# A gated mix of attention and feed-forward on one core: first transposing transfers whole, another duration and another set of weights in the planner

## The chip, the core and the metric

The kernel runs on one core of a Trainium2 chip. A core has a matrix engine (TensorE, in the profile PE, its weight loads PEld), a vector engine (VectorE, DVE), an activation engine (ScalarE, ACT), a general engine (GpSimd, POOL) and SyncE (SP), which here only issues transfers. Sixteen DMA engines move data between main memory and the on-chip memory. Results of PE land in PSUM, which the kernel uses as eight banks of 128 partitions by 512 float32 columns. The metric is the device time of one launch in microseconds.

## The reference

Sequence 2048, width 512, 32 heads of 16, feed-forward width 1792, all in bfloat16. The inputs named `B_x` and `A_x` are both given, and only `A_x` is read.

```
g = sigmoid((x * gate_w).sum(-1, keepdims=True))
q, k, v = split of x @ wqkv, 32 heads of 16
a = softmax(q @ k.T / 4) @ v, heads joined, @ wo
b = (silu(x @ w_gate) * (x @ w_up)) @ w_down
out = g * a + (1 - g) * b
```

The attention scores are 32 x 2048 x 2048 values, and each goes through an exponential. That is 2048 banks of 128 by 512.

## The kernel before, in words

**Units, slots and tiles.** The work of attention is cut into 32 units: a block of 512 queries and a group of four heads. A unit has 16 slots, one for each block of 128 keys. The scores of one slot are one tile: four banks, one for each of four heads. There are 512 slots, and `plan.slot` counts them.

**Two ways for a tile.** Most tiles are ACT's: PE computes two banks of scores (`score`), ACT takes the exponential of both in one instruction into `e_all` (`emit_group`, list `exps`), and PE multiplies the result by the values (`pv`), accumulating in one bank per unit. The other tiles are DVE's. It evicts the scores bank by bank with a multiplication and an addition into 16-bit integers whose bits read as a bfloat16 approximate an exponential (`emit_d`, tiles `c_t`; some lie in the space of `kaug` and `wd_t`). A sharper approximation needs several such images. With `groups[n] == 4` three shifted copies are made of the first (`copy`; the first of them on POOL, `lifted`), and PE makes four passes over the values. With `groups[n] == 2` two masks and a product are made (`bits`, `product`), and PE makes two passes. POOL can take a copy or a product from DVE (`take_over`), and works only beside certain instructions of DVE (`beside`).

**The planner.** The program is written by a planner in Python that runs when the kernel is built. It holds a clock for each engine (`plan.pe`, `plan.act`, `plan.dve`, `plan.pool`) and adds a fixed duration for each instruction that it emits. The order on every engine is the order of emission (`ordered`). `later(cost, f, ...)` puts a piece of DVE's work into the list `owed`, with the duration that the planner counts for it. `choose` picks which PSUM banks get the next group of scores, `v_unit` decides whether a tile of the present or next unit goes to DVE, `side` whether a piece of the projections or of the feed-forward goes to PE. The feed-forward, the projections of later units and the output run as such pieces beside attention.

**The weights.** These decisions are governed by 31 numbers. `begin(n)` replaces all of them at the slots that are keys of the table `WEIGHTS`:

```
HUNGRY, KEEP, FED, W3, W3T, W4, W4T, W4B, N1, N2, LOW, EXTRA, NEXT, SPARE, BURST, SHORT, BACK, FIRST, EB, OWN, NY, TAKE_C, TAKE_P, GLEAD, WINDOW, FACE, LATEST, SLACK, LEAD, LINE, STACK = WEIGHTS[n]
```

Until the first key, the constants at the head of the function hold. Those that the prediction names: `EB` is the number of pairs of banks in `e_all` after which PE must first multiply by values; `LEAD` is the time before the end of a unit's exponentials by which DVE must be able to begin a tile; `STACK` is the DVE work that may stand in the queue when another tile is taken; `TAKE_C` and `TAKE_P` let POOL take a copy or a product from DVE; `WINDOW` and `GLEAD` are the time that POOL must have for it.

**The start.** ACT's DMA queue loads 64 columns each of the weights and half of the plain rows of x; SP's loads the other rows and then issues the transposing transfers into `xT`, which holds x turned, in four chunks of 128 columns. For rows 0 to 1023 only chunks 0 and 1 come by such transfers; chunks 2 and 3 are turned by PE from the plain rows in `wd_t` (`turn`). Then come chunks 0 to 3 of rows 1024 to 2047. After these SP issues the rest of the value and projection weights. PE, after twelve matmuls that keep it going, turns its chunks, computes the keys and queries of the first unit in the order of chunks 3, 0, 2, 1 (rows 0 to 511, then 512 to 1023), bounds the scores, and starts with the first scores. The keys of rows 1024 to 2047 follow as planned pieces (`k0_pieces`).

**The gate.** `gate_end`, a piece at about slot 106, takes the exponential of 128 by 16 numbers on ACT and then has five small operations on DVE.

Of the kernel before, what the change touches and what calls it, by code (L numbers as in the profile page):

```python
# [82 lines left out]
def kernel(  # L83
# [13 lines left out]
    P = 128  # L97
    x = A_x.flatten_outer_dims()
# [6 lines left out]
    DC = D // P  # L105
    FC = F // P
    KT = S // P
    QBW = 512
# [10 lines left out]
    EB = 9  # L119
# [143 lines left out]
    def act(out, in_, **kw):  # L263
        ordered(nc.scalar.activation(out=out, in_=in_, **kw), [in_, *kw.values()], [out])  # L264
# [17 lines left out]
    queue = Ordered(nc.sync)  # L282


    xT = big.tile([P, DC, S], BF16, name="xT")
    wd_t = big.tile([P, FC, D], BF16, name="wd_t")
    HALF = DC // 2
    x_rows = wd_t[:, 0:4, :].rearrange("p f d -> p (f d)").rearrange("p (i d) -> p i d", d=HALF * P)
    def rows(q, t0):
        q.dma_start(out=x_rows[:, TQ * t0:TQ * t0 + TQ, :], in_=x[t0 * QBW:(t0 + 1) * QBW, HALF * P:D].rearrange("(i p) d -> p i d", p=P))  # L290

    def turned(dc, t0, n):
        queue.dma_start_transpose(out=xT[:, dc, t0:t0 + n * QBW], in_=x[t0:t0 + n * QBW, dc * P:(dc + 1) * P])

    rows(queue, 0)
    for t0 in (0, QBW):
        for dc in range(HALF):
            turned(dc, t0, 1)
    for dc in range(DC):
        turned(dc, 2 * QBW, 2)  # L300
    wqk = big.tile([P, DC, 2 * D], BF16, name="wqk")
    for c0 in (D, 0):
        if c0 == 0:
            rows(nc.scalar, 1)
        nc.scalar.dma_start(out=wqk[:, :, c0:c0 + 64],
                            in_=A_wqkv[:, c0:c0 + 64].rearrange("(dc p) c -> p dc c", p=P))
# [5 lines left out]
    for c0 in (D, 0):  # L312
        queue.dma_start(out=wqk[:, :, c0 + 64:c0 + D],
                          in_=A_wqkv[:, c0 + 64:c0 + D].rearrange("(dc p) c -> p dc c", p=P))
# [98 lines left out]
    plan = Plan()  # L413
# [4 lines left out]
    held = [None] * NP  # L418

    LANDED = 6.9  # L420
    FLIP, UNIT_US, PIECE_US, COLS_US, TURN = 0.1055, 0.2157, 0.0024, 0.2133, 0.0105
    TO_ACT, ACT_FIX, ACT_COL, ACT_IN = 0.485, 0.064, 0.4265, 0.167
    ACT_PE, DVE_PE, PE_DVE, ACT_DVE = 0.055, 0.08, 0.24, 0.06
    GPS = 1
    OWN = 0
    POOL_IN, POOL_FIX, POOL_ONE, POOL_PE, POOL_OVER = 0.12, 0.12, 0.43, 0.2, 0.1
    TAKE_P = 1
    FACE = 1
    TAKE_C = 1
    GLEAD = 5.771  # L430
    SLACK = 0.04
    LEAD = 7.615
    LINE = 1.3
    STACK = 4.9
    WINDOW = 1.503

    def spend(mode, mms, ready=0.0):

        plan.seq += 1
        work_at.append((plan.pe, mms))  # L440
        plan.pe = max(plan.pe + (FLIP if mode != plan.mode else 0.0), ready) + (TURN if mode == "C" != plan.mode else 0.0) + (0.226 * mms if mode == "F" else PIECE_US + COLS_US * mms)
        plan.mode = mode

    def later(cost, f, ready=None, key=None, fast=False):

        c = plan.chain
        if c is not None:
            c.owed += 1
        ready = plan.pe + PE_DVE if ready is None else ready
        owed.insert(sum(o[0] <= ready for o in owed), (ready, cost, f, c, key, fast))  # L450
# [318 lines left out]
    def gate_end():  # L769
        act(out=ge[:, :], in_=ge[:, :], func=ACT.Exp, scale=-1.0)  # L770
        plan.act += 0.2

        def end():
            vec.tensor_scalar(out=omg[:, :], in0=ge[:, :], scalar1=1.0, scalar2=None, op0=ALU.add)
            vec.reciprocal(gval[:, :], omg[:, :])
            vec.tensor_tensor(out=omg[:, :], in0=ge[:, :], in1=gval[:, :], op=ALU.mult)
            vec.reciprocal(odds[:, :], ge[:, :])
            wide.append(work.tile([P, QBW], BF16, tag="rd", name="rd")[:, :].bitcast(F32))
            vec.tensor_copy(out=wide[0][:, 0:P], in_=ident[:, :])
        later(0.5, end, plan.act + ACT_DVE, fast=True)  # L780
# [94 lines left out]
    def e_run(w):  # L875

        used = set(e_slot.values())
        for k in range(NE):
            i = (e_next[0] + k) % NE
            if i + w <= NE and not any(j in used for j in range(i, i + w)):  # L880
                return i
        return None
# [15 lines left out]
    def choose():  # L898
# [51 lines left out]
        left = (hi[au] - at_) * 4 - quarter  # L950
        if left >= 4 and len(e_slot) // 2 + 2 <= EB and e_run(4) is not None and not exps:
            for n in range(min(want, 2) + 1):
# [145 lines left out]
    def home_at(n):  # L1098

        short = n // KT > closed and any(v > 0 and m // KT == closed for m, v in needs.items())  # L1100
        return sorted(c_free)[1 if short else 0]
# [110 lines left out]
    def until(n):  # L1212

        un = n // KT
        return plan.act + (hi[au] - at_) * TILE_US + (hi[un] * TILE_US if un > au else 0.0)

    def take_over():

        seen = set()
        for i, (_, _, _, n, _, what) in enumerate(vops):  # L1220
            first = n not in seen
            seen.add(n)
            if what is None or n // KT < au:
                continue
            if what[0] == "P" and TAKE_P and first and n not in jobs and plan.dve + 2 * NV * WINDOW + GLEAD <= until(n):
                _, h, y = what
# [3 lines left out]
                return n  # L1230
            if what[0] == "C" and TAKE_C and what[1] == 2 and plan.dve + (NV + (len(jobs[n][4]) if n in jobs else 0)) * WINDOW + GLEAD <= until(n) and home_at(n) <= plan.dve:
                _, k, h, y = what
# [546 lines left out]
    for qb in range(QB):  # L1779
        for b in range(NB):  # L1780
# [21 lines left out]
            for g in {max(2 * b, 1), 2 * b + 1}:  # L1802
                q_of[UNIT.index((qb, g))] = q
    gates = [pace.add([(0.2, gate_end, False)], 40, 106, v_rest)]
    turned = pace.add([(1, turn_odds, True, "F", None)], 40, 130, gates, 2)
    need.setdefault(160, []).append(turned)

    def first_loads():
# [130 lines left out]
    def begin(n):  # L1939
        nonlocal HUNGRY, KEEP, FED, W3, W3T, W4, W4T, W4B, N1, N2, LOW, EXTRA, NEXT, SPARE, BURST, SHORT, BACK, FIRST, EB, OWN, NY, TAKE_C, TAKE_P, GLEAD, WINDOW, FACE, LATEST, SLACK, LEAD, LINE, STACK  # L1940
        plan.slot = n
        if n in WEIGHTS:
            HUNGRY, KEEP, FED, W3, W3T, W4, W4T, W4B, N1, N2, LOW, EXTRA, NEXT, SPARE, BURST, SHORT, BACK, FIRST, EB, OWN, NY, TAKE_C, TAKE_P, GLEAD, WINDOW, FACE, LATEST, SLACK, LEAD, LINE, STACK = WEIGHTS[n]
        for c in need.get(n, []):
            force(c)
        if n == 3:
            queue.dma_start(out=gw_col[:], in_=gate_w.rearrange("(dc p) -> p dc", p=P))
        if n == 28:
            late_loads()
        i = n - (QB + 1) * KT - 8  # L1950
        if 0 <= i < 2 * FC and i % 4 == 0:
            wd_due.append(i // 2)
        while wd_due and (wd_due[0] >= 4 or not wd_home[0]):
            wd_load(wd_due.pop(0))
        for f in at.pop(n, []):
            f()
        pace.begin_slot(n)
# [43 lines left out]
    def next_pv():  # L2001
        flush_act()
        while not pv_list(None):
            if d_wait:
                pay_d()
            elif vops and c_ready() < 1e9:
                pay_v()
            elif owed:
                pay()
            elif workable(1e8) is not None:  # L2010
                lifted(workable(1e8))
            elif asides:
                aside_now()
            else:
                lone_d()
        emit_pv(pv_list(None)[0])
# [19 lines left out]
    def v_unit():  # L2036
# [4 lines left out]
        while vu < UNITS:  # L2041
# [3 lines left out]
            if vu >= au and left > 0 and (vu or hi[0] > KT // 2):  # L2045
                end = plan.act + (left - 1) * TILE_US + ((hi[au] - at_) * TILE_US if vu > au else 0.0)
                busy = sum(v[0] for v in vops) + 0.6 * len(owed) + sum(d[3] for d in d_wait)
                if plan.dve + busy + (LEAD if vu < UNITS - 1 else LAST) <= end:
                    return vu
# [32 lines left out]
    while au < UNITS:  # L2082
# [5 lines left out]
        back = len(e_slot) // 2  # L2088
        if back >= EB or e_run(3) is None:
            next_pv()  # L2090
# [10 lines left out]
        if room > 0.02:  # L2101
# [4 lines left out]
            col = c is not None and (c.pieces[c.i][3:] or "C")[0] == "C"  # L2106
            urgent = c is not None and c.deadline < 0 and back < EB - 4
            visit = len(n_pv) + (len(c.pieces) - c.i if col else 0)
            going = col and 0 < c.i and len(c.pieces) < SHORT and back < EB - BACK
            if n_pv and fits > 0 and not urgent and not going and (plan.mode == "C" or visit > 1 and fits > 1 and (pv_turn[0] or c is None or col)  # L2110
# [119 lines left out]
```

## Time and profile before

| | |
|---|---|
| median of 3 runs | 746.43 us (746.19 to 746.45) |
| profiled execution | 747.79 us |
| its span, first to last instruction | 746.1 us |
| ACT busy | 731.5 us, 98% |
| PE busy | 731.6 us, 98% |
| DVE busy | 712.9 us, 96% |
| POOL busy | 281.6 us, 38% |
| granted clock of PE | 1.00 |

A row of the profile's groups reads: line, engine, operation, tile written and tiles read with their shapes, count, then busy time in us and mean duration of one in ns, then the idle time of the engine just before them and what ended it. Busy time of a group is a union: instructions of one engine overlap, so the mean times the count can be more. A row of the chain of waits reads: start, length, what. Nearly all instructions have the line of a helper (L261 for PE, L264 for ACT, L277 for the others), so groups are told apart by their tiles.

### The profile page before, as it was taken

The numbers are of one execution on the slowest core, as the hardware profiler recorded it, in microseconds if no ns is written. First come the engines' busy times: TensorE is split into PE (matmuls) and PEld (weight loads), VectorE is DVE, ScalarE is ACT, GpSimd is POOL, SyncE is SP. The second block draws the span as 40 slices with busy tenths as digits, with TensorE's granted clock in tenths as the row PEclk, the third lists the DMA queues.
The fourth block names the chain that finished last, engine by engine and source line by source line (L and its number), as shares of the span: only waits on it lengthen the run. The fifth ranks groups of instructions, "written<-read, shape, count | busy, mean of one in ns | idle before, by whom it ended". The sixth has DMA issues, their size and how long they took to land.

```text
span 746.1 us, 24177 instructions
## 1 busy us (share of the span) xinstructions
PE 731.6 (98%) x10198; PEld 238.8 (32%) x10198; DVE 712.9 (96%) x1175; ACT 731.5 (98%) x828; POOL 281.6 (38%) x400
## 2 busy tenths in 40 slices
PE   7999999999999999999999999999999999999997
PEld 3333233333333333333333333333332333333332
DVE  6799999999999999999999999999999999999995
ACT  5999999999999999999999999999999999999996
POOL 7034432442533412544323444442245235443320
PEclk9999999999999999999999999999999999999999
DMA  9010211353220003131100131211000132100011
GB/s 197 10 44 15 58 30 35 68 136 73 65 49 14 8 20 96 45 71 38 38 17 13 40 102 36 64 35 46 18 26 16 48 94 60 33 17 16 14 31 37
DMA packets 91685, 34.92 MB, mean 47 GB/s; under 512 B 75761, under 2 KB 91129, under 8 KB 91577
## 3 DMA queue, kind: packets, MB, share of 16 engines
q1 hardware_dynamic: 89320, 32.79, 18.6%
q8 instruction: 80, 1.31, 0.8%
q10 hardware_dynamic: 2256, 0.59, 0.4%
q14 instruction: 29, 0.23, 0.1%
HBM read 21.55 MB, written 2.35 MB: 32 GB/s over the span
## 4 chain that ended last, share of the span: by engine, by line
ACT 57%; PE 32%; DVE 6%; SPq 1%; issue 1%; DMA 1%; POOL 0%; DVEq 0%; POOLq 0%
ACT e_all L264 55%; PE psum L261 32%; DVE c_t L277 4%; ACT th L264 2%; SPq L277 1%; DMA xT<-in_A_x_dram 1%; DVE kaug L277 1%; DVE mt L277 1%; DVE gs L277 0%; DMA wu<-in_B_w_up_dram 0%; DVE on L277 0%; DMA on<-osb 0%; DVE osb L277 0%; POOL c_t L277 0%; DVEq L2225 0%
## 5 line engine op out<-in xcount | busy, mean ns | idle before, releaser
L264 ACT ACTIVATE e_all<-psum 128x1024 bf16<-128x1024 f32 (+1 forms) x755 | 706.7, 1103 | 2.6 <-PE psum L261 2.4
L277 DVE TENSOR_SCALAR c_t<-psum 128x512 uint16<-128x512 f32 x454 | 300.9, 684 | 8.6 <-PE psum L261 6.8
L261 PE MATMUL psum<-qx,kaug 32*128 32x512 bf16 (+1 forms) x1632 | 243.1, 385 | 4.2 <-ACT e_all L264 2.9
L277 POOL TENSOR_TENSOR c_t<-c_t,lift 128x256 int32<-128x256 int32 (+1 forms) x162 | 114.7, 716 | 169.3 <-DVE c_t L277 129.0
L261 PE MATMUL psum<-e_all,vaug 128*32 128x512 bf16 (+3 forms) x1992 | 164.9, 332 | 0.0
L261 PEld LDWEIGHTS <-kaug 32*128 32x128 bf16 (+1 forms) x2048 | 74.6, 91 | 262.2 <-ACT e_all L264 181.1
L261 PE MATMUL psum<-c_t,vaug 128*32 128x512 bf16 (+3 forms) x1856 | 144.1, 332 | 0.6 <-DVE kaug L277 0.3
L261 PEld LDWEIGHTS <-vaug 128*32 128x32 bf16 x4144 | 98.8, 95 | 125.5 <-issue 86.0
L277 DVE TENSOR_SCALAR c_t<-c_t 128x2048 uint16<-128x2048 uint16 (+2 forms) x194 | 131.5, 685 | 1.1
L277 POOL TENSOR_TENSOR c_t<-c_t 128x256 bf16<-128x256 bf16 (+3 forms) x62 | 53.9, 882 | 82.6 <-DVE c_t L277 57.4
L261 PE MATMUL psum<-xT,wg 128*32 128x512 bf16 x896 | 73.6, 383 | 0.1
L261 PE MATMUL psum<-wd_t,mt 128*32 128x512 bf16 x896 | 72.9, 383 | 0.0
L261 PE MATMUL psum<-xT,wu 128*32 128x512 bf16 x896 | 71.7, 383 | 0.1
L261 PE MATMUL psum<-q,kaug 32*128 32x512 bf16 (+1 forms) x256 | 48.6, 385 | 0.1
L277 POOL TENSOR_TENSOR kaug<-c_t,lift 128x256 int32<-128x256 int32 (+1 forms) x38 | 26.3, 701 | 43.2 <-DVE c_t L277 35.2
L261 PE MATMUL psum<-xT,wqk 128*32 128x512 bf16 x512 | 41.0, 383 | 0.2 <-DVE c_t L277 0.2
L277 DVE TENSOR_SCALAR kaug<-psum 128x512 uint16<-128x512 f32 x60 | 39.9, 680 | 0.8 <-PE psum L261 0.7
L277 DVE TENSOR_TENSOR c_t<-c_t 128x2048 bf16<-128x2048 bf16 (+1 forms) x32 | 39.1, 1222 | 0.0
L277 DVE SCALAR_TENSOR_TENSOR gs<-th,psum 128x512 bf16<-128x512 bf16 x56 | 37.9, 677 | 1.2 <-ACT th L264 1.1
L277 DVE SCALAR_TENSOR_TENSOR mt<-gs,psum 128x512 bf16<-128x512 bf16 x56 | 37.9, 677 | 1.0 <-PE psum L261 0.5
L264 ACT ACTIVATE th<-psum 128x512 bf16<-128x512 f32 x56 | 37.8, 674 | 0.0
L277 POOL TENSOR_TENSOR aq<-aq,kb 128x256 bf16<-128x256 bf16 x32 | 19.5, 612 | 47.4 <-DVE c_t L277 36.7
(127 smaller groups left out, 480.0 us busy)
## 6 DMA issues: line engine op xcount, KB each, us to landing
wg<-in_B_w_gate_dram SPq DMA_DIRECT2D x56, 128.0 KB
wu<-in_B_w_up_dram SPq DMA_DIRECT2D x56, 128.0 KB
on<-osb SPq DMA_DIRECT2D x120, 16.0 KB
rb<-rr SPq DMA_DIRECT2D x15, 128.0 KB
wd_t<-in_B_w_down_dram SPq DMA_DIRECT2D x7, 256.0 KB
qx<-qst SPq DMA_DIRECT2D x96, 16.0 KB
qx<-aq SPq DMA_DIRECT2D x96, 16.0 KB
out_dram<-o_t SPq DMA_DIRECT2D x12, 128.0 KB
```

The lines of the kernel that those rows point to most:

```text
L261: return ordered(nc.tensor.matmul(out, lhsT=lhsT, rhs=rhs, **kw), [lhsT, rhs], [out])
L264: ordered(nc.scalar.activation(out=out, in_=in_, **kw), [in_, *kw.values()], [out])
L277: return ordered(f(*a, **kw), reads, [out])
```

## The change

Three parts. The first four transposing transfers, 512 rows each, become two of 1024 rows; the four that follow stay as they are, so that SP issues six instead of eight. The planner counts 1.1 us instead of 0.5 for the five operations of the gate's end on DVE; the operations stay. The table of weights is another: 96 tuples, the first at slot 4, instead of 54 from slot 8; three tuples (at 88, 184 and 344) are in both tables. The opening constants `EB`, `GLEAD` and `LEAD` differ, too.

```
-    EB = 9
+    EB = 8
...
-    WEIGHTS = {8: (0, 0, 5.918, -0.267, -0.106, 0.5, 0.1, 0.1, 5.912, 0.508, 1.233, 0.818, 1.035, 0.271, 8.958, 18, 2, 0.339, 8, 1, 3, 0, 1, 0, 1.3, 0, 0.64, 0.02, 5.778, 1.771, 4.9),
...
+    WEIGHTS = {4: (0.08, 2, 4.965, -0.428, 0.009, 4, 0.248, 0.189, 6.643, 2.494, 1.557, 0.742, 0.94, 0.637, 8.802, 12, 2, 0.171, 8, 0, 3, 1, 1, 5.099, 1.444, 1, 0.605, 0.036, 7.295, 1.3, 4.9),
+        8: (0.08, 2, 4.965, -0.493, 0.009, 4, 0.302, 0.189, 6.643, 2.494, 1.557, 0.742, 0.898, 0.637, 8.802, 12, 2, 0.022, 8, 1, 3, 1, 1, 5.099, 1.444, 1, 0.605, 0.036, 7.295, 1.3, 4.9),
...
-    def turned(dc, t0, n):
-        queue.dma_start_transpose(out=xT[:, dc, t0:t0 + n * QBW], in_=x[t0:t0 + n * QBW, dc * P:(dc + 1) * P])
-
     rows(queue, 0)
-    for t0 in (0, QBW):
-        for dc in range(HALF):
-            turned(dc, t0, 1)
-    for dc in range(DC):
-        turned(dc, 2 * QBW, 2)
+    for t0 in (0, 2 * QBW):
+        for dc in range(DC if t0 else HALF):
+            queue.dma_start_transpose(out=xT[:, dc, t0:t0 + 2 * QBW], in_=x[t0:t0 + 2 * QBW, dc * P:(dc + 1) * P])
...
-    GLEAD = 5.771
+    GLEAD = 4.671
     SLACK = 0.04
-    LEAD = 7.615
+    LEAD = 7.295
...
-        later(0.5, end, plan.act + ACT_DVE, fast=True)
+        later(1.1, end, plan.act + ACT_DVE, fast=True)
```

The means over slots 8 to 511, each tuple held until the next key, of the fields that the prediction uses: `LEAD` 5.61 before and 4.50 after, `STACK` 4.72 and 5.39, `TAKE_C` 0.38 and 0.53, `TAKE_P` 0.91 and 0.81, `WINDOW` 1.48 and 1.30.

2 lines of the change are left out of this document (1 added, 1 removed).

## The prediction

> **What bounds the kernel now.** I read the page's totals first, then the busy time of the long middle stage, then the chain of waits, then the groups of instructions kept apart by shape, and last the first 20 us instruction by instruction.
>
> ```profile
> PE 731.6 (98%) x10198; PEld 238.8 (32%) x10198; DVE 712.9 (96%) x1175; ACT 731.5 (98%) x828; POOL 281.6 (38%) x400
> ```
>
> ```profile
> 20.00:737.00 717.00, 711.55 (x9993) 229.88 (x9994) 696.94 (x1126) 716.69 (x807) 267.17 (x368) 1.00 0.18 43
> ```
>
> The totals don't separate PE, ACT and DVE. The stage row does (columns: stretch and length, then busy time and count of PE, PEld, DVE, ACT, POOL, then granted clock, DMA share, GB/s). Between 20 and 737 us ACT is busy 716.69 of 717.00 us, so 0.31 us of it is idle. DVE has 20.06 us idle there.
>
> ```profile
> 31.73 0.51 ACT mt L264
> ...
> 389.54 39.35 ACT e_all L264 x43
> 428.88 0.10 issue
> 428.98 1.08 ACT e_all L264
> 430.06 0.49 ACT th L264
> ```
>
> A busy engine can still be stretched by waits inside its instructions; these chain rows (start, time, what) say it isn't. 43 exponentials in a row end every 39.35 / 43 = 0.915 us, and a tanh of the feed-forward part adds 0.49.
>
> ```profile
> L264 ACT ACTIVATE e_all<-psum 128x1024 bf16<-128x1024 f32 x749 | 700.4, 1098 | 2.6 <-PE psum L261 2.4
> L264 ACT ACTIVATE e_all<-psum 128x1536 bf16<-128x1536 f32 x6 | 9.7, 1623 | 0.0
> L277 DVE TENSOR_SCALAR c_t<-psum 128x512 uint16<-128x512 f32 x452 | 298.5, 681 | 8.6 <-PE psum L261 6.8
> L277 DVE TENSOR_SCALAR kaug<-psum 128x512 uint16<-128x512 f32 x60 | 39.9, 680 | 0.8 <-PE psum L261 0.7
> L277 DVE TENSOR_SCALAR wd_t<-psum 128x512 uint16<-128x512 f32 x16 | 10.7, 681 | 0.2 <-PE psum L261 0.2
> L277 DVE TENSOR_SCALAR c_t<-psum 128x1024 uint16<-128x1024 f32 x2 | 2.4, 1221 | 0.0
> ```
>
> The exponentials are divided between two engines. ACT takes 749 x 2 + 6 x 3 = 1516 banks of 512 columns. DVE takes 452 + 60 + 16 + 2 x 2 = 532 banks, which is 133 tiles of four. Together they are 2048 banks, all of them. So ACT's length is set by one number, how many tiles the planner gives to DVE. One tile more on DVE takes two double exponentials from ACT: 2 x 0.915 = 1.83 us. Nothing else in the middle stage can move the time by more than the 0.31 us that ACT idles, unless it makes ACT wait anew.
>
> The rest is 20 us at the start and 9 at the end:
>
> ```profile
> 7.85 1.30 SPq L277
> ...
> 9.20 1.30 SPq L277
> ...
> 10.54 5.40 DMA xT<-in_A_x_dram
> ...
> 15.98 0.96 PE psum L261 x10
> ...
> 16.96 14.77 ACT e_all L264 x16
> ```
>
> ```profile
> 1.33 1.23 SPq L277
> ...
> 2.61 1.25 SPq L277
> ...
> 3.90 1.26 SPq L277
> ...
> 5.20 1.26 SPq L277
> ```
>
> The chain begins with SP issuing eight transposing transfers one after another. The last is issued from 10.54 us, its data are whole at 15.94, PE stands until then, and ACT stands for PE.
>
> **The change, part by part.** *First transfers whole.* The first four transposes (512 rows each) become two of 1024 rows. A short one costs SP 1.23 to 1.26 us to issue, a long one 1.30 (rows above), so the issue price hardly knows the size. Four short ones occupy 1.33 to 6.47; two long ones would need 2 x 1.34 = 2.68, and every later issue on SP moves up by about 5.18 - 2.68 = 2.5 us. Behind them on SP stand the other four transposes and then the loads of the value and projection weights, which also move up. What the last landing is worth is bounded by who waits:
>
> ```profile
> 11.93 2.99 ACT L264 ACTIVATE e_all<-psum 128x1024 bf16<-128x1024 f32 x3 [0.17 <-PE psum L261]
> 16.96 14.77 ACT L264 ACTIVATE e_all<-psum 128x1024 bf16<-128x1024 f32 x16 [2.04 <-PE psum L261]
> ```
>
> ACT stands still for 2.04 us; that is the most this part can give, even though the issue moves by 2.5. Against it stands the earlier use:
>
> ```profile
> 6.19 0.45 PEld L261 LDWEIGHTS <-wd_t 128*128 128x128 bf16 x8 [0.16 <-DMA wd_t<-in_A_x_dram]
> 7.23 2.76 PE L261 MATMUL psum<-xT,mt 128*128 128x512 bf16 x16 [0.42 <-ACT xT L264]
> ```
>
> ```profile
> 4.00:6.00 2.00, 2.00 (x14) 1.01 (x12) 1.45 (x7) 0.68 (x3) 1.96 (x9) 1.00 1.26 216
> 6.00:8.00 2.00, 1.58 (x16) 0.91 (x14) 1.86 (x3) 1.42 (x3) 1.72 (x8) 1.00 0.90 155
> ```
>
> At 7.23 us PE starts on the transposed x and runs 16 matmuls without a stop. With whole transfers its second and fourth matmul need data of rows 512 to 1023 to have landed as well. The DMA engines are full at that time (share 1.26, then 0.90), and the doubled packets also sit beside the load of plain rows that PE waits for at 6.19. I bound the delay of the first exponential by 0 and by 0.7 us (half of the 1.3 us that one long transfer occupies) and take 0.2. If the last landing moves up by only half of 2.5 us, 1.25 are won instead of 2.04. So the start gives between -2.04 and +0.7; I take -1.5, nearest to the row of ACT's wait less the small delay.
>
> One rule speaks against that part. The Trainium skill, "DMA: Bandwidth & Descriptors", section "Issuing engines are not separate DMA queues", says that all issuers feed the same 16 engines and that the sequencer's time to start a transfer is usually small beside the transfer. By that, the saved issues would bring nothing here, the sum would lack the 1.5 us, and the time would be 742.6. The issue rows above show 1.23 to 1.30 us each and back to back, so I hold the queue of issues to be the limit, with the full DMA share as the reason for a doubt.
>
> *Gate's end.* The planner counts 1.1 us of DVE instead of 0.5 for five small operations:
>
> ```profile
> 167.18 0.16 DVE L277 TENSOR_SCALAR omg<-ge 128x16 f32<-128x16 f32 x1
> ...
> 168.00 0.68 DVE L277 TENSOR_SCALAR c_t<-psum 128x512 uint16<-128x512 f32 x1
> ```
>
> ```profile
> 170.00:175.00 5.00, 4.80 (x6) 1.00 0.00 0
> ```
>
> They held DVE from 167.18 to 168.00, 0.82 us. The instructions are the same after the change; only the order planned around them moves. The later stall that can be charged to it is the 0.20 us that ACT idles in 170 to 175. Worth 0 to -0.2; I take -0.1. What covers it otherwise is the stock of banks in front of ACT.
>
> *Buffers at the outset.* EB 8 for 9 holds only until the first tuple, at slot 4, and the opening constants are otherwise those of before except for two lead times. Nothing in the first stall depends on them: 0.
>
> *The weights.* They say how many tiles go to DVE and what a tile costs there.
>
> ```profile
> L261 PE MATMUL psum<-e_all,vaug 128*32 128x512 bf16 x1108 | 107.3, 383 | 0.0
> L277 DVE TENSOR_SCALAR c_t<-c_t 128x2048 uint16<-128x2048 uint16 x189 | 129.5, 692 | 1.1
> L277 DVE TENSOR_SCALAR kaug<-c_t 128x2048 uint16<-128x2048 uint16 x34 | 23.4, 690 | 0.1
> L277 DVE TENSOR_SCALAR c_t<-kaug 128x2048 uint16<-128x2048 uint16 x30 | 20.8, 697 | 0.2
> L277 DVE TENSOR_TENSOR c_t<-c_t 128x2048 bf16<-128x2048 bf16 x31 | 38.0, 1227 | 0.0
> L277 POOL TENSOR_TENSOR c_t<-c_t 128x512 bf16<-128x512 bf16 x22 | 25.4, 1156 | 22.3 <-DVE c_t L277 18.5 <-DVE kb L277 2.2 <-DMA on<-osb 1.3
> L277 POOL TENSOR_TENSOR c_t<-c_t 128x256 bf16<-128x256 bf16 x38 | 25.3, 670 | 56.8 <-DVE c_t L277 38.8 <-DVE kaug L277 15.5 <-DVE aq L277 2.0
> ```
>
> The four eviction rows further up (351.5 us), the three copy rows here (173.7) and the product row (38.0) make 563.2 us for 133 tiles, 4.2 us of DVE each. DVE's 20.06 idle microseconds hold at most 20.06 / 4.2 = 4.8 more tiles if nothing gets cheaper. Holding each tuple until the next key, I average the fields over slots 8 to 511, from the diff: LEAD, the time before a unit's end at which no further tile may be taken, falls from 5.61 to 4.50 us; STACK, the DVE work that may be queued, rises from 4.72 to 5.39; TAKE_C, POOL taking over a copy that costs DVE 0.69 us, is on in 53% of the slots instead of 38%; WINDOW, what POOL's share must fit, falls from 1.48 to 1.30. All four let DVE start more tiles or do them cheaper. TAKE_P, POOL taking over a product of 1.23 us, goes the other way, from 91% to 81%.
>
> No row shows how many tiles come of this. The bounds are +5 (all idle time of DVE, with a copy or two on POOL) and, below, -3 (the ten products that POOL does now in the two rows above, (22 x 2 + 38) / 8, all back on DVE: 10 x 1.23 / 4.2). I take +2: about half of the idle time (10 us, 2.4 tiles), since much of the other half is DVE's wait for PE before evictions (6.8 + 0.7 + 0.2 us in the eviction rows), which the weights needn't lift. That is -2 x 1.83 = -3.7 us. On PE a tile costs one or three more passes against the values; a pass is four matmuls side by side of 0.38 us (the PE row), so two tiles cost at most 6 x 0.38 = 2.3 us, and PE has 717.00 - 711.55 = 5.45 us idle in the stage row.
>
> *Sum.* -1.5 - 0.1 - 3.7 = -5.3 us. The profiled execution took 747.79 us (span 746.1), 1.36 more than the median 746.43; it may have had a longer wait at the start than the timed ones, which is a second reason to take 1.5 of 2.04. On its own time the sum gives 742.5, on the median 741.1.
>
> **The rivals.** *Transfers bound the start, not issues.* For it: the DMA share of 0.90 to 1.26 in the rows above. Against it: long issues at an even 1.34 us spacing. The start then gives 0: 746.43 - 3.8 = 742.6.
>
> *The division stays at 133.* For it: ACT without a gap and DVE with only 2.8% idle leave little. Against it: four fields loosened. Only the start and the gate count: 746.43 - 1.6 = 744.8.
>
> *DVE's tiles get dearer, slower.* With TAKE_P off in more slots, products come back from POOL to DVE, 1.23 us each. Seven of them, 8.6 us, cost DVE two tiles, and ACT 3.7 us: 746.43 - 1.6 + 3.7 = 748.5. It decides once more than six come back, with no other gain: (1.6 + 1.5) / 1.83 = 1.7 tiles, 7.1 us of DVE, 5.8 products. For it: POOL products fill 50.7 us of those two rows today, so there is something to lose. Against it: TAKE_C moves work the other way.
>
> **How the numbers follow.** Forecast 0.45; transfer-bound start with two tiles 0.17; division unchanged 0.14; dearer tiles 0.20; one tile fewer, 746.6, 0.04. A measurement of this kernel can tell about 0.2%, 1.5 us, from no change: faster is below 744.9, slower above 747.9. Unchanged division lies on that bound; I give 0.08 of it to faster and 0.06 to same. Faster 0.45 + 0.17 + 0.08 = 0.70, same 0.10, slower 0.20. Low end: five tiles and the whole wait, 746.43 - 9.2 - 2.0 = 735.2. High end: two tiles fewer, 748.5. Outside I leave about 0.15: three or more tiles fewer 0.10, more than five tiles 0.05.
>
> **What would show it.** The eviction rows should add up to about 540 banks instead of 532, and the double exponentials to about 745 instead of 749. SP's issues should show six transposes, the last from about 8 us, and ACT's idle time before the exponential now at 16.96 should fall from 2.04 to about 0.5. ACT should stay busy for all but a few tenths of the middle stage. The prediction is wrong if ACT idles there by more than a microsecond, if the count of banks on DVE falls, or if the first exponential comes more than 0.7 us after 11.93.

## The result, and the profile after

The changed kernel takes 745.09 us (median of 20 runs), the one before 746.28 us beside it: a ratio of 0.9986, 95% interval 0.9980 to 0.9992. That is 1.2 us faster, 0.14%, within the 0.2% that the prediction calls no change. The forecast was 5.3 us. A second series with the same kernel (`after_again`) gave 745.07 against 746.29 (0.9983, 0.9974 to 0.9991), so the 1.2 us is firm. One of the twenty runs of the kernel before took 1543 us and stands outside the ratio.

The profiled executions differ by more: 747.79 us (span 746.1) before, 745.10 (span 743.4) after. The one of before was 1.5 us above its median, the one after lies on it. What the two traces differ by at the start is therefore not what the timed runs differ by.

The stage rows of the kernel after (stretch, length, busy time and count of PE, PEld, DVE, ACT, POOL, clock, DMA share, GB/s), then its groups by shape:

```profile
20.00:733.00 713.00, 710.02 (x10038) 231.00 (x10034) 697.43 (x1126) 712.83 (x801) 272.87 (x388) 1.00 0.18 43
```

```profile
L264 ACT ACTIVATE e_all<-psum 128x1024 bf16<-128x1024 f32 x747 | 696.1, 1080 | 0.3 <-PE psum L261 0.2
L264 ACT ACTIVATE e_all<-psum 128x1536 bf16<-128x1536 f32 x6 | 9.2, 1540 | 0.0
L277 DVE TENSOR_SCALAR c_t<-psum 128x512 uint16<-128x512 f32 x462 | 308.1, 684 | 7.4 <-PE psum L261 5.3
L277 DVE TENSOR_SCALAR kaug<-psum 128x512 uint16<-128x512 f32 x64 | 42.6, 684 | 0.4 <-PE psum L261 0.2
L277 DVE TENSOR_SCALAR wd_t<-psum 128x512 uint16<-128x512 f32 x8 | 5.4, 683 | 0.1
L277 DVE TENSOR_SCALAR c_t<-psum 128x1024 uint16<-128x1024 f32 x1 | 1.2, 1220 | 0.0
```

ACT is still busy without a gap, 712.83 of 713 us. It takes 747 x 2 + 6 x 3 = 1512 banks instead of 1516; DVE takes 462 + 64 + 8 + 2 = 536 instead of 532. So the new table gives DVE 134 tiles: one more, not two.

The start after, as ACT, SP and PE show it (start, length, what, idle time before):

```profile
1.34 9.90 SPq L277 DMA_TRANSPOSE xT<-in_A_x_dram  x6
11.28 0.58 SPq L277 DMA_DIRECT2D rb<-in_A_wqkv_dram  x1
```

```profile
4.12 3.08 SPq L277 DMA_TRANSPOSE xT<-in_A_x_dram  x1
```

```profile
7.34 0.62 PE L261 MATMUL psum<-ident,wd_t 128*128 128x128 bf16 x8 [0.26 <-DMA wd_t<-in_A_x_dram]
7.80 2.80 PE L261 MATMUL psum<-xT,mt 128*128 128x512 bf16 x16
```

```profile
12.53 17.52 ACT L264 ACTIVATE e_all<-psum 128x1024 bf16<-128x1024 f32 x19 [0.16 <-PE psum L261]
```

Six issues take SP 9.90 us (9.57 to 9.98 in the six executions with two whole transfers and all loads); the eight of before took 10.50. The two saved issues are nearly all eaten by one: the third holds SP for 3.08 us instead of 1.30. (In `t_only`, below, it is the second, with 2.60 us.) The plain rows that PE turns come later, PE starts its first block at 7.80 instead of 7.23, and the first exponential at 12.53 instead of 11.93. In exchange ACT no longer stops before its fourth.

Worked out from the traces of all runs: when ACT starts its first and its fourth exponential, how long from the start of the fourth to the end of the last one, the numbers of double and triple exponentials (g_only and w_only have a single one besides), and what is left of that length when each double counts 0.917 us and each triple 1.344 (and a single 0.49), the usual distances from end to end. The remainder is the tanh of the feed-forward, a few small operations and ACT's waits. The runs are described in the next section.

```
kernel        first starts  fourth starts  to the end of the last  doubles  triples  remainder
before               11.93          16.96                  721.26      749        6       26.4
gate_out             12.31          15.24                  721.04      749        6       26.1
t_only               13.26          15.98                  721.27      749        6       26.4
after                12.53          15.26                  719.97      747        6       26.9
after_again          12.36          15.09                  719.95      747        6       26.9
no_t                 12.31          15.92                  720.07      747        6       27.0
no_t_again           12.37          15.12                  720.25      747        6       27.2
rows_first           12.69          15.41                  720.08      747        6       27.0
no_rows              11.57          14.30                  720.05      747        6       27.0
t_2048               15.43          18.15                  719.95      747        6       26.9
one_less             12.47          15.20                  721.80      749        6       26.9
two_less             12.75          15.47                  723.76      754        4       27.0
g_only               12.03          15.68                  734.28      758        5       32.0
w_only               12.30          15.08                  735.74      765        3       29.7
```

In the middle stage the change is worth 721.26 - 719.97 = 1.29 us: 1.83 from one tile, less about 0.5 of ACT's waits. That is as much as the measured gain. It repeats: the seven executions with the changed table and gate and all their tiles lie at 719.95 to 720.25, `before`, `t_only` and `gate_out` at 721.04 to 721.27.

At the start the 16.96 of before stands alone. The five other executions with eight short transfers (`no_t`, `no_t_again`, `gate_out`, `g_only`, `w_only`) start the fourth exponential at 15.08 to 15.92 us, the six with two whole ones (`t_only`, `after`, `after_again`, `rows_first`, `one_less`, `two_less`) at 15.09 to 15.98.

### The profile page after: what moved, and what is told of

Its sections match the earlier page's. It is cut to its first block, busy times and chain, and to the rows that moved or that the text cites. A ratio compares the mean times of both kernels' runs of the same rounds, so it can differ in the third digit from the quotient of the medians.

```text
span 743.4 us, 24397 instructions
## 1 busy us (share of the span) xinstructions
PE 733.5 (99%) x10293; PEld 241.2 (32%) x10294; DVE 714.4 (96%) x1175; ACT 730.3 (98%) x826; POOL 287.3 (39%) x420
## 4 chain that ended last, share of the span: by engine, by line
PE 49%; ACT 48%; DMA 1%; issue 1%; DVE 0%; DVEq 0%; ACTq 0%
PE psum L261 49%; ACT e_all L264 47%; ACT th L264 1%; DMA wd_t<-in_A_x_dram 1%; DVE c_t L277 0%; ACT mt L264 0%; DVE mt L277 0%; DVEq L2220 0%; ACTq L300 0%; DVE rt L277 0%; ACT ge L264 0%
## 5 line engine op out<-in xcount | busy, mean ns | idle before, releaser
L277 DVE TENSOR_SCALAR c_t<-psum 128x512 uint16<-128x512 f32 x463 | 309.3, 685 | 7.4 <-PE psum L261 5.3
L277 POOL TENSOR_TENSOR c_t<-c_t,lift 128x256 int32<-128x256 int32 (+2 forms) x223 | 154.1, 701 | 244.6 <-DVE c_t L277 182.2
L261 PEld LDWEIGHTS <-vaug 128*32 128x32 bf16 x4240 | 103.0, 95 | 124.3 <-issue 84.1
L277 DVE TENSOR_SCALAR c_t<-c_t 128x2048 uint16<-128x2048 uint16 (+2 forms) x182 | 122.9, 682 | 1.5
L277 POOL TENSOR_TENSOR c_t<-c_t 128x256 bf16<-128x256 bf16 (+1 forms) x38 | 33.7, 899 | 65.3 <-DVE c_t L277 40.3
L277 DVE TENSOR_SCALAR kaug<-psum 128x512 uint16<-128x512 f32 x64 | 42.6, 684 | 0.4 <-PE psum L261 0.2
L277 DVE TENSOR_TENSOR c_t<-c_t 128x2048 bf16<-128x2048 bf16 x28 | 34.3, 1224 | 0.0
L261 PEld LDWEIGHTS <-mt 128*32 128x32 bf16 (+1 forms) x1044 | 23.7, 96 | 26.9 <-issue 21.0
L277 POOL TENSOR_TENSOR c_t<-kaug,lift 128x256 int32<-128x256 int32 (+1 forms) x31 | 22.5, 735 | 23.9 <-DVE c_t L277 21.5
```

The source lines that it names most:

```text
L261: return ordered(nc.tensor.matmul(out, lhsT=lhsT, rhs=rhs, **kw), [lhsT, rhs], [out])
L277: return ordered(f(*a, **kw), reads, [out])
```

## Experiments

**The transfers by themselves, and the change without them.** `t_only` is the kernel before with this edit alone; `no_t` is the changed kernel with the edit undone.

```
-    for t0 in (0, QBW):
-        for dc in range(HALF):
-            turned(dc, t0, 1)
-    for dc in range(DC):
-        turned(dc, 2 * QBW, 2)
+    for t0 in (0, 2 * QBW):
+        for dc in range(DC if t0 else HALF):
+            queue.dma_start_transpose(out=xT[:, dc, t0:t0 + 2 * QBW], in_=x[t0:t0 + 2 * QBW, dc * P:(dc + 1) * P])
```

> The kernel before with only the four short transposing transfers made two whole ones; weights and gate as before, so 133 tiles and 1516 banks on ACT, order of all engines unchanged. Prediction's step (issue-bound): ACT's wait before its fourth exponential falls from 2.04 us to about 0.5, 1.5 us faster, 744.8. Theory now (the changed kernel's trace): the third transfer's issue holds SP about 3.1 us instead of 1.3, because two whole transfers are already outstanding, so the last issue moves up by about 0.6 us only; the plain rows of x land later and the first exponential comes at about 12.5 us instead of 11.9; the wait before the fourth exponential falls to about 0. In timed runs, where the wait of before looks like 0.8 us rather than 2.3, that is -0.2 us, 746.1.

> The changed kernel with the four short transfers of before; 134 tiles, 1512 banks on ACT. Prediction's step: 1.5 us slower than the changed kernel, 746.6. Theory now: first exponential back at 11.9 us, a wait of 0.4 to 2 us before the fourth; in the timed runs +0.2 us, 745.3. If the start matters nothing, the whole gain of 1.2 us over before comes from one tile more (1.83 us) less some waits of ACT in the middle stage.

`t_only`: 746.20 us beside 746.30 (ratio 0.9995, 0.9986 to 1.0005). The forecast of 744.8 is out. `no_t`: 745.61 beside 746.30 (0.9988, 0.9978 to 0.9998), and in a later series:

> The changed kernel with the four short transfers once more, to size the transfers' share: its median was 745.6, the changed kernel's 745.1 in two other jobs. If whole transfers are worth 0.5 us, it is 745.6 again, 0.999 of before; if that was chance, 745.1, 0.9985.

745.59 beside 746.45 (0.9984, 0.9975 to 0.9992). The changed kernel was at 0.9986 and 0.9983. By medians the whole transfers may be worth up to 0.5 us in the changed kernel and 0.1 in the old one; by the ratios nothing can be told from zero. The trace of `t_only`, its chain of waits at the start, shows why there is so little:

```profile
1.34 1.30 SPq L277
2.65 0.05 issue
2.69 6.47 DMA xT<-in_A_x_dram
9.16 0.04 issue
9.21 2.13 PE psum L261 x13
...
13.26 12.02 ACT e_all L264 x13
```

Here PE waits for the second whole transfer itself, which lands 6.47 us after its issue began; the first exponential comes 1.3 us later than before. This execution was the slowest of its eleven (746.78 us), so its delay may be larger than the usual one. And in `no_t` the old wait, with the old transfers, is small:

```profile
12.31 1.94 ACT L264 ACTIVATE e_all<-psum 128x1024 bf16<-128x1024 f32 x2 [0.17 <-PE psum L261]
14.55 1.02 ACT L264 ACTIVATE e_all<-psum 128x1024 bf16<-128x1024 f32 x1 [0.29 <-PE psum L261]
15.92 14.77 ACT L264 ACTIVATE e_all<-psum 128x1024 bf16<-128x1024 f32 x16 [0.35 <-PE psum L261]
```

ACT idles 0.29 and 0.35 us before its third and fourth exponential, not the 2.04 us of the profile before. With the same eight transfers the fourth exponential starts at 15.92 here and at 16.96 there, so a microsecond of that wait belonged to that one execution. In the second execution, `no_t_again`, there is no wait at all:

```profile
12.37 10.29 ACT L264 ACTIVATE e_all<-psum 128x1024 bf16<-128x1024 f32 x11 [0.16 <-PE psum L261]
```

The landings on record say what was special. A transposing transfer is marked as landed by sixteen updates of its semaphore. For the last transfer of before, fifteen of them had come by 14.18 us, and the sixteenth came at 15.94, 1.76 us later. In the five other traces with eight short transfers the sixteenth came 0.01 to 0.15 us after the fifteenth, at 14.06 to 14.90. So the wait of 2.04 us on which the prediction built was one late part of one transfer in one execution. Why that part was late, nothing here shows.

**What holds the third issue.** Two ideas: a limit on how many transposes may be outstanding, or DMA engines that are full. `no_rows` takes 256 KB out of the DMA engines and leaves all transposes. It turns rows 0 to 511 twice in place of rows 512 to 1023, so chunks 2 and 3 of the latter are wrong; every engine does the same work.

```
-        if c0 == 0:
-            rows(nc.scalar, 1)
...
-            mm(ps[k // TQ][:, k % TQ * P:(k % TQ + 1) * P], lhsT=x_rows[:, k, (dc - HALF) * P:(dc - HALF + 1) * P],
+            mm(ps[k // TQ][:, k % TQ * P:(k % TQ + 1) * P], lhsT=x_rows[:, k % TQ, (dc - HALF) * P:(dc - HALF + 1) * P],
```

> The changed kernel without the load of the plain rows 512 to 1023 of x on ACT's queue (256 KB); PE turns the rows 0 to 511 a second time in their place, so chunks 2 and 3 of rows 512 to 1023 are wrong and the output with them; all engines do the same work. If the transfers bound the start (the sixteen DMA engines full between 2 and 14 us), 256 KB less, at the 216 GB/s of the row of 4 to 6 us, frees 1.2 us: the six issues end at about 10.0 us instead of 11.2, and the first exponential comes at about 11.7. If SP is held by a limit on outstanding transposes, the long issue stays at about 3 us and SP ends at about 11.2 as in the changed kernel. On the time: transfer-bound 744.3, limit on transposes 744.5 to 745.1.

Its third issue, all six, and its first exponentials:

```profile
4.21 1.45 SPq L277 DMA_TRANSPOSE xT<-in_A_x_dram  x1
```

```profile
1.33 8.35 SPq L277 DMA_TRANSPOSE xT<-in_A_x_dram  x6
```

```profile
11.57 2.85 ACT L264 ACTIVATE e_all<-psum 128x1024 bf16<-128x1024 f32 x3 [0.16 <-PE psum L261]
```

744.35 us, against 745.07 for the changed kernel beside it. The long issue is gone, 1.45 us instead of 3.08, and SP is done 1.56 us earlier. A limit of two outstanding whole transposes would have kept it: here the third was issued by 5.66 us, before the first had landed at 6.23. So the length of the issue depends on what other loads move at the same time. That it is the full DMA engines that hold SP is argued, not shown; parts of transfers that leave a queue more slowly beside other loads would look the same. The DMA share (it adds up the times of packets and can pass 1) goes with it: in the row of 6 to 8 us the changed kernel has 1.40, where the profile before had 0.90 and `no_t`, with the same transfers as before, 1.21. But from 4 to 6 us both have 1.26, so the share alone doesn't tell a long issue from a short one:

```profile
4.00:6.00 2.00, 2.00 (x6) 0.69 (x5) 1.45 (x7) 0.67 (x3) 1.95 (x9) 1.00 1.26 219
6.00:8.00 2.00, 1.74 (x19) 1.20 (x18) 1.41 (x2) 0.82 (x2) 1.67 (x8) 1.00 1.40 177
```

The earlier first exponential of `no_rows`, 11.57 us, proves less. The load that it leaves out is the one that the chain to the first exponential runs through in the changed kernel:

```profile
1.31 5.98 DMA wd_t<-in_A_x_dram
```

`t_2048` goes the other way, one transfer of 2048 rows for each of chunks 0 and 1, four issues in all:

```
+    for dc in range(DC):
+        t0 = 0 if dc < HALF else 2 * QBW
+        queue.dma_start_transpose(out=xT[:, dc, t0:S], in_=x[t0:S, dc * P:(dc + 1) * P])
```

> The changed kernel with chunks 0 and 1 brought by one transfer of 2048 rows each, four issues instead of six. If the long issue in the changed kernel comes from too many rows outstanding, the second or third issue here takes 3 us or more, SP is done with its transposes at about 11 us again, and nothing of the two saved issues is gained. If the price is per issue (the prediction), four issues end at about 6.6 us. In either case rows 0 to 1023 land later, and the first exponential comes 1 us or more after 12.5.

A single run, 748.12 us. Four issues take 9.75 us, the first 2.92 of them and the second 4.09, and PE waits for the second one's data; its chain of waits:

```profile
1.33 2.92 SPq L277
4.25 0.05 issue
4.30 6.78 DMA xT<-in_A_x_dram
11.08 0.04 issue
11.12 2.38 PE psum L261 x13
...
15.43 10.19 ACT e_all L264 x11
```

The first exponential is 2.9 us later than after, the time 3.0. Eight issues, six and four of the same bytes took SP 10.50, 9.90 and 9.75 us. So a fixed price per issue does not carry over to fewer and larger transfers. With eight issues it may still be what sets SP's pace: none was shorter than 1.23 us in any trace.

`rows_first` tried to win back the first exponential by putting the plain rows ahead of the key weights on ACT's queue.

```
-        if c0 == 0:
+        if c0 == D:
             rows(nc.scalar, 1)
```

> The changed kernel, but ACT's queue issues the plain rows 512 to 1023 of x before the 64 columns of the key weights. If the late landing of those rows (about 7.3 us instead of 6.1) is what delays the first exponential, it comes back from 12.5 to about 12.0 us and the kernel gains 0.5 us: 744.6. If the transposed rows themselves are what PE waits for at about 7.8 us, the first exponential stays at 12.5 and the time at 745.1. If the key weights become late by it, the first exponential comes later than 12.5.

745.69 us beside 746.30 (0.9989, 0.9979 to 0.9999): 0.6 more than the changed kernel by medians, nothing that the ratios can tell. ACT now waits 2.62 us for the key weights, before the operation that pads them, and the first exponential comes at 12.69. What one load wins here, another loses: the plain rows land at 4.87 us instead of 7.30, the key weights at 6.77 instead of 4.71.

```profile
6.86 0.44 ACT L264 ACTIVATE mt<-wqk 128x256 bf16<-128x256 bf16 x1 [2.62 <-DMA wqk<-in_A_wqkv_dram]
```

**Is a tile worth 1.83 us, and is it ACT's count that binds?** Two kernels give up one and two tiles late in the program by raising one field, LEAD, of one tuple.

```
one_less: in the tuple at slot 484
-    LEAD 4.626
+    LEAD 8.626
two_less: in the tuple at slot 436
-    LEAD 4.416
+    LEAD 6.416
```

> The changed kernel once more, beside the next three on one chip: 745.1 us, 0.9985 of before.

> The changed kernel with LEAD raised by 4.0 us in the one tuple at slot 484 (4.626 to 8.626). As built it has 133 tiles on DVE, one fewer, and the plan is the same before slot 484. Theory: ACT has two double exponentials more and waits no more than before: 2 x 0.917 = 1.8 us slower than the changed kernel, 746.9. Rival, that the middle stage is set by DVE or PE rather than by ACT's count (they are 98% and 99% busy, too): a tile fewer relieves DVE of 4.2 us, and the time does not rise, 745.1 or less.

> The changed kernel with LEAD raised by 2.0 us in the one tuple at slot 436 (4.416 to 6.416). As built it has 132 tiles, two fewer. Theory: 3.7 us slower than the changed kernel, 748.8. Rival as for one_less: not slower.

745.07, 746.50 and 750.18 us. In `one_less` the exponentials are those of the kernel before, 749 doubles and 6 triples, and DVE's evictions make 133 tiles:

```profile
L264 ACT ACTIVATE e_all<-psum 128x1024 bf16<-128x1024 f32 x749 | 697.9, 1082 | 0.3 <-PE psum L261 0.2
L277 DVE TENSOR_SCALAR c_t<-psum 128x512 uint16<-128x512 f32 x454 | 302.2, 683 | 7.4 <-PE psum L261 5.3
L277 DVE TENSOR_SCALAR kaug<-psum 128x512 uint16<-128x512 f32 x68 | 45.2, 683 | 1.0 <-PE psum L261 0.9
```

From the fourth exponential to the end of the last, the tables' rows say 1.83 us more for one tile and 3.79 for two (754 doubles and 4 triples make 3.7). The rival, that DVE or PE binds and a tile fewer costs nothing, is out. This is shown for tiles late in the program, at slots 484 and 436. The whole times rose by 1.4 and 5.1: the stretch after the last exponential differs from kernel to kernel, 7.82 us in `one_less` and 8.72 in `two_less`, and it was 8.15 and 9.23 in two executions of the changed kernel itself. In `two_less` some 0.7 us more lies outside the span from first to last instruction (748.0 of 750.43 us, where the kernel after has 743.4 of 745.10); what it is, the trace doesn't show.

**Gate and weights apart.** `g_only` is the kernel before with the gate's end counted as 1.1; `w_only` has the new table and opening constants with the gate's end at 0.5 and the eight transfers of before.

```
g_only:
-        later(0.5, end, plan.act + ACT_DVE, fast=True)
+        later(1.1, end, plan.act + ACT_DVE, fast=True)
w_only:
-    EB = 9
+    EB = 8
-    WEIGHTS = {8: (0, 0, 5.918, ...
+    WEIGHTS = {4: (0.08, 2, 4.965, ...
-    GLEAD = 5.771
+    GLEAD = 4.671
-    LEAD = 7.615
+    LEAD = 7.295
```

> The kernel before with only the gate's end counted as 1.1 us by the planner; weights and transfers as before. The instructions of the gate are the same. Prediction's step: worth 0 to -0.2 us, so 746.1 to 746.3. Theory now: the old weights fit one plan to the instruction, and any other duration from slot 106 on throws the rest of the plan off. The program as built has 129 tiles on DVE instead of 133, so ACT has 8 double exponentials more, 8 x 0.917 = 7.3 us: at least 753.6; and if the orders that no longer fit make ACT wait too, up to 759. Told apart by the trace: 755 + 8 exponentials, and the idle time of ACT between 20 us and the end.

> The kernel before with only the new weights (and the opening constants with them); the gate's end is still counted as 0.5 us. Prediction's step: LEAD, STACK, TAKE_C and WINDOW loosen what DVE may take, two tiles more, 746.3 - 3.7 = 742.6, since the gate is worth only 0.1. Theory now: the new weights fit only the plan in which the gate counts 1.1; as built this program has 127 tiles, 6 fewer than before, 12 exponentials more, 11.0 us: at least 757.3, and up to 761 with waits of ACT.

759.77 us (1.0182, 1.0165 to 1.0199) and 760.84 us (1.0193, 1.0177 to 1.0208): either half alone is 13.4 and 14.5 us slower than the kernel before beside it (746.38), both together, in `no_t` and `no_t_again`, 0.7 and 0.9 faster than the one beside them. `w_only` gives DVE 127 tiles and ACT 765 doubles. `g_only` gives DVE 129 tiles, and its order makes ACT wait as well; two rows of ACT:

```profile
689.83 1.95 ACT L264 ACTIVATE e_all<-psum 128x1024 bf16<-128x1024 f32 x2
694.88 5.61 ACT L264 ACTIVATE e_all<-psum 128x1024 bf16<-128x1024 f32 x6 [3.10 <-PE psum L261]
```

The remainders in the table, 32.0 and 29.7 instead of 26.4, are such waits: 5.6 and 3.3 us. The rest is the count: 16 and 24 banks more on ACT.

**What the gate's end costs on the chip.** `gate_out` keeps the plan of before (0.5) and leaves out three of the five operations; `gval` and `odds` are constants instead, so the output is not the reference's.

```
-            vec.reciprocal(gval[:, :], omg[:, :])
-            vec.tensor_tensor(out=omg[:, :], in0=ge[:, :], in1=gval[:, :], op=ALU.mult)
-            vec.reciprocal(odds[:, :], ge[:, :])
...
+    nc.gpsimd.memset(gval[:], 0.5)
+    nc.gpsimd.memset(odds[:], 1.0)
```

> The kernel before, planned as before (gate's end 0.5 us), but three of the gate's five operations on DVE (both reciprocals and the product) are left out; their results are constants set at the start, so the output is wrong. The other instructions and their order stay. In the traces of before and of t_only ACT waits 0.30 us at 174.4 us, 6 us behind the gate's end; in the changed kernel it doesn't. If the five operations, 0.82 us long against 0.5 planned, cause that wait, it is gone here and the time is 0.3 us less than before, 746.0; 133 tiles as before. If it has another cause in the order of the engines there, it stays at 0.30 us, and the gate's end is worth nothing by itself.

745.98 us beside 746.45 (0.9993, 0.9984 to 1.0002). The time can't tell; the trace can. The exponential that came 0.30 us late at 174.4 us in before is 0.06 late here, and ACT has no idle time in that stretch:

```profile
170.00:175.00 5.00, 5.00 (x72) 1.68 (x68) 5.00 (x10) 5.00 (x6) 1.23 (x2) 1.00 0.00 0
```

So the three operations of the gate's end, which was longer than planned, did cost about 0.24 us. The 0.30 us is the same in the traces of before and `t_only`; the 0.06 is from one. (The profile's rows show it as 0.20 us idle, since instructions of ACT overlap; 0.30 is by the distance of the ends.)

## Why the prediction was right or wrong

**What binds.** Right. ACT's count of banks sets the middle stage in every kernel tried, and 1.83 us for a tile is what `one_less` shows. All variants lie on that count plus their waits: the remainder is 26.1 to 27.2 us where the plan fits, and 32.0 and 29.7 in the two kernels with half of the change.

**The step "first transfers whole", -1.5 us.** Wrong, and this is the first of two mis-sized terms. It took the price of an issue, 1.23 to 1.30 us, as fixed, and let the later issues move up by 2.5 us. That was read from rows of short issues; with whole transfers the third issue takes 3.08, and SP's last transposing issue begins at 9.93 us instead of 10.54, not at about 8. The measured worth is between 0 and 0.5 us. The outcome is that of the first rival, a start worth nothing because transfers and not issues bound it: `no_rows` and `t_2048` show that fewer bytes shorten the issues and fewer issues of the same bytes don't shorten the start. The sentence of the Trainium skill, "DMA: Bandwidth & Descriptors", section "Issuing engines are not separate DMA queues", that the time to initiate is usually small beside the transfer, pointed the right way. The runs agree with it in the outcome: eight, six and four issues of the same bytes took 10.50, 9.90 and 9.75 us; how short an issue could be by itself they don't show. The delay of the first exponential, taken as 0.2 within 0 to 0.7, was 0.6 in the profile after, and 1.3 in that of `t_only`, which is outside the bounds. The 11.93 of before was itself early: the other traces with eight short transfers have 12.03 to 12.37.

A second error sits in the same term, and it alone undoes it. ACT's wait of 2.04 us was taken from an execution 1.36 us above the median. The prediction named this as a reason for caution and then still used three quarters of it. In the five other traces with the same eight transfers ACT stands for 0 to 0.68 us before its third and fourth exponential together (0.64 in `no_t`), so there was little to win whatever the issues cost.

**The step "the weights", +2 tiles, -3.7 us.** That the table acts through the number of tiles is right, and so is the price of a tile; the number is off: +1 tile, -1.83 us. Reading the averages of LEAD, STACK, TAKE_C and WINDOW as more or fewer tiles was the weak link. A single LEAD does what was said: raised at one slot, it loses a tile. But the table as a whole can't be read that way. With these same averages `w_only` gave up six tiles, so that the sign of the forecast came true was luck. The numbers fit one plan to the instruction, and another duration of 0.6 us from slot 106 on undoes them.

**The gate's end, -0.1.** As a cost on DVE it was sized about right: ACT's wait of 0.30 us at 174.4 is gone after, and about 0.24 of it was the gate's, by `gate_out`. As an edit it was costed wrongly at nearly nothing: alone it costs 13.4 us, since everything planned after it moves. "Only the order planned around them moves" was the sentence that should have been priced.

**Waits of ACT.** The text gave 0.31 us of ACT's idle time as the most that the middle stage could move "unless it makes ACT wait anew". It does, a little: the exponentials' lateness against 0.917 us, summed between 20 us and the end with early ones counted off, is 0.97 us before and 1.49 after. Nine waits of 0.08 to 0.17 us between 338 and 689 us, 1.06 us in all, are new; gone are the 0.30 us at 174.4, one of 0.22 and two of 0.06. PE's idle time fell with it, from 5.45 of 717 us to 2.98 of 713; that PE's fuller order causes these waits is argued, not tested.

**The rivals.** "The division stays at 133" missed by one tile, and its 744.8 is close to the measured time by two errors that cancel: no tile and 1.6 us at the start, where it was one tile and next to nothing. "Tiles get dearer" did not happen. Products on DVE cost 54.0 us now; in the groups before they were 56.1. Of these the prediction counted only the largest row, 38.0, in its 4.2 us of DVE for a tile; with all products and copies it is 4.4, which changes little.

**The signs that were named.** None of the three that were to prove the prediction wrong appeared: ACT idles 0.17 us in the middle stage, DVE's banks rose, and the first exponential came 0.6 us later. What missed were the counts expected: 536 banks instead of about 540, 747 doubles instead of about 745, and the last transposing issue.

**The sum again**, with what was measured: -1.83 for the tile, +0.5 for waits, 0 to -0.5 for the start, and +0.3 after the last exponential (8.15 us against 7.85, which varies by a microsecond from run to run). That is -1.0 to -1.5; measured -1.2. How much of the half microsecond at the start is the transfers' is left open.

## What to carry to other kernels

Where several engines are all at 96% or more, look for the one whose instructions follow each other end to end; then count what it does, and price a change in units of that count. A table of numbers fitted to a planned program has to be judged by the program that it makes, not by where its averages moved: half of a matched change can cost ten times what the whole brings. Before a saved issue is counted as time, ask what else the DMA engines have to move at that moment; and take no wait from one profiled execution that is slower than its own median without a second trace, and look at whether the last part of the transfer it waits for came with the others.

## What the runs showed that was not expected

The issue of a transposing transfer is elastic: 1.23 to 1.27 us for 512 rows in six executions; for 1024 rows about 1.3 in most places, but 2.81 to 3.10 as the third of the changed kernel in four executions (`after`, `after_again`, `one_less`, `two_less`) and 1.45 there without half of the plain rows; 2.92 and 4.09 for two of 2048 rows. One late part of sixteen, 1.76 us behind the others, made ACT's wait of 2.04 us in the profile before. ACT's exponentials of 1024 columns followed each other at 0.917 us from end to end, within 0.02 us in 97 to 99% of them (98.7% before, 97.9% after), over 700 us, in a kernel whose PE and DVE were 96 to 99% busy, too.
